# A Fourier mixer with a routed expert layer on one core: constant matmuls in TensorE's idle time, and one selection fewer

## The chip, the cores and the metric

One NeuronCore of a Trainium2 chip runs the whole program. The metric is device time in microseconds (us) for one execution, lower is better. Timings of the same program are repeated; the median of three runs stands for it.

## What is computed

For each of 8 batches, `x[b]` is a 3136 x 256 float32 array. It goes through a Fourier layer with a soft threshold, and then 128 of its 3136 rows go through an expert:

```python
X = rfft(x, axis=1)
Yr = Xr @ w_r - Xi @ w_i + b_r
Yi = Xr @ w_i + Xi @ w_r + b_i
Y = shrink(Yr, 0.01) + 1j * shrink(Yi, 0.01)
y = irfft(Y, n=3136, axis=1)
scores = y[b] @ w_gate
top = the 128 rows with the largest scores
out[b] = y[b]
out[b, top] += sigmoid(scores[top]) * (relu(y[b, top] @ w1) @ w2)
```

w1 is 256 x 1024 and w2 is 1024 x 256.

## The kernel before

**Stages of a batch.** 3136 is split as 98 x 32. In the first transform (`s1`, eight pieces a batch) DVE or POOL makes sums `xu` and differences `xv` of the input tile `xt`; TensorE (PE) multiplies them by the constant `first` into PSUM banks `s`; the result is stored to DRAM as `As`. In the second transform (`s2`, six passes a batch) PE multiplies the reloaded tile `av` by the constant `second` into `px0` and `px1`; ACT and DVE split the result into a high part `Xh` and a low part `Xl`. Eight spectral products (`spectral`, three matmuls each, with the weights `wh` and `wl`) follow each pass, into a bank `py`. `shrink` is the threshold. `s2i` (six a batch) and `s2it` transform back, and DVE takes the dot product with the gate at the same time (`score_part`, into `Csc`); the result goes to DRAM as `Cs`, comes back as `cin`, and eight `s1i` pieces a batch end the transform and store the output `out`.

**Routing.** `score(b)` brings a batch's scores into one tile. `select(bs, bits, lag)` (L516) finds the 128th largest score of each batch of a group by a search over the bits of the float: with bits = 3 there are twelve rounds. In a round DVE compares all scores with the candidates (tile `c`), counts (tile `n`), PE adds the counts over partitions by a product with ones (`px<-n,tm`), and DVE picks the digit from it (`digest`). Each step waits for the one before. After the last round come the mask, prefix sums on PE, one-hot rows (`hot`) and the row numbers `idxs`. `GROUPS` (L1032) says which batches are selected together; each group waits for the scores of all its batches and for the group before (`route`, L1088 to L1093).

**Expert.** For each batch POOL gathers 128 rows (`xe`, L643); PE turns them (`prepare`), multiplies by w1 in two halves of 16 matmuls (`hidden`), ACT and DVE make high and low parts, PE does 24 matmuls with w2 (`combine`), DVE adds (`ye`), and POOL scatters the rows (`out`, L723). Two threads of `ffn` can be at work after the last spectral product; before it, one.

**What sets the order.** The program is written out by a planner that runs while the kernel is built. It keeps a planned time for each engine (`free`), for each tile and for the DMA wire, and the order it writes is the order in which each engine's queue runs on the chip. `pe["end"]` is when PE's last planned matmul ends. The main loop (L1241 to L1295) takes, at each step, the PE work that costs least: a wait plus a penalty for being early or late in the plan (L1269 to L1273); selection and expert threads have a fixed rank, and `FIL` is the price of an expert step, first before and then after the end of the spectral products. `pump` writes the work of the other engines up to a planned time, which lies `AHEAD` (late in the program, `AHEADT`) in front of PE. `EARLY` lets a load from DRAM scratch be put in SP's queue that much before the store it needs is planned to land. `LOWA` and `DB` hold DVE's selection steps back while the spectral products run, `TD` does so for threads at the end (L1062 to L1072). `spec["t"]` counts passes of spectral products; T = 48 is all of them; `at` is 0 until the first product is written.

Of the kernel before, what the change touches and what calls it, by code (L numbers as in the profile page):

```python
# [10 lines left out]
F32 = mybir.dt.float32  # L11
# [8 lines left out]
B, S, D = 8, 3136, 256  # L20
# [141 lines left out]
def fourier_moe(ctx: ExitStack, tc: tile.TileContext, x, w_r, w_i, b_r, b_i, wg, w1, w2,  # L162
# [6 lines left out]
    ps = ctx.enter_context(tc.tile_pool(name="ps", bufs=2, space=bass.MemoryType.PSUM))  # L169
# [4 lines left out]
    free = dict.fromkeys(("PE", "DVE", "ACT", "POOL", "SP"), 0.0)  # L174
    done, read, base, where = {}, {}, {}, {}
    pe = {"mode": None, "end": 0.0}
# [81 lines left out]
    def mm(out, a, b, start=True, stop=True, at=(0, 0)):  # L258
        k, m, n = b.shape[0], out.shape[0], int(np.prod(b.shape[1:]))
        mode = (32 if k <= 32 else 64, 64) if k <= 64 and m <= 64 else (128, 128)  # L260
        t = begin("PE", [out], [a, b])
        if mode != pe["mode"]:
            t = max(t, pe["end"]) + 0.13
        c = max(n * (1.68 if b.dtype == F32 else 0.45), (220 if b.dtype == F32 else 110) if mode[0] == 128 else 28) / 1000
        own = [(r, q) for r in range(at[0] // 32, (at[0] + mode[0]) // 32) for q in range(at[1] // 32, (at[1] + mode[1]) // 32)]
        t = max([t] + [cells.get(x, 0.0) for x in own])
        for x in own:
            cells[x] = t + c
        pe["mode"], pe["end"] = mode, max(pe["end"], t + c)
        free["PE"] = max(free["PE"], t + 0.012)  # L270
        finish("PE", [out], [a, b], t + c + 0.15)
        return nc.tensor.matmul(out, a, b, start=start, stop=stop)  # L272
# [37 lines left out]
    def new(p, shape, dt, name, bufs=2):  # L310
        ring = rings.setdefault((name,), Ring(bufs))
        assert ring.bufs == bufs
        old = None
        if len(ring.tiles) >= bufs:
            old, holds = ring.tiles.pop(0)
            for g in holds:
                drain(g)
        t = p.tile(shape, dt, name=name, bufs=bufs)
        if old is not None:
            base[key(t)] = max(done.get(old, 0.0), read.get(old, 0.0))  # L320
        where[key(t)] = "ps" if p is ps else "sb"
        ring.tiles.append((key(t), []))
        return t

    def open_at(name, count=1):

        ring = rings.get((name,))
        if ring is None:
            return 0.0
        n = count - (ring.bufs - len(ring.tiles))  # L330
        t, v = 0.0, free["DVE"]
        for o, holds in ring.tiles[:max(n, 0)]:
            t = max(t, done.get(o, 0.0), read.get(o, 0.0))
            for s in holds:
                if not s.over:
                    v = max(v, s.when()) + 0.55
                    t = max(t, v)
        return t
# [66 lines left out]
    first = c_tile([128, 2, 2, 64], F32, "first")  # L405
# [3 lines left out]
    wh, wl = [c_tile([128, 2, 2, 2, D], F32R, n) for n in ("wh", "wl")]  # L409
# [27 lines left out]
    made = set()  # L437
# [5 lines left out]
    def consts_s():  # L443
        yield "SP", behind_a(CA[0])
        ld(sec[0].rearrange("p j s -> p (j s)"), t_second[:, :NJ * 64])
        yield "SP", behind_a(CA[3])
        ld(tail, t_tail)
        yield "SP", behind_a(CA[4])
        ld(wgb, wg.rearrange("(o e) -> o e", o=1).broadcast_to([128, D]))
        ld(sec[1].rearrange("p j s -> p (j s)"), t_second[:, NJ * 64:])  # L450

    def consts_w():
        yield "SP", behind_a(CA[1])
        ts = []
# [12 lines left out]
    def consts_bias():  # L467
        vec.memset(m2l, -2.0 * LAM)
        yield "SP", behind_a(CA[2])
        for c, src in enumerate((b_r, b_i)):  # L470
# [274 lines left out]
    def x_side():  # L745

        for b in range(B):
            for i in range(8):
                if b:
                    if b == 1:  # L750
                        yield "SP", behind_a(CA[5])
                    o = (b, i - XB) if i >= XB else (b - 1, i + (0 if b == 1 else XB))
# [262 lines left out]
    MX, SB = False, 4  # L1015
    Q = 6
    T = B * Q
    AVB = 2
    YP = (1,)
    R0 = 2  # L1020
    EARLY, AHEAD, SW = 0,1.1,0.2
    BACK, TAIL = 99,40
    LAST = 3
    PF = (0,0.3)
    BEGIN, RATE, DB = 2.5,2.2,0.3
    LOWA = 0.4
    AHEADT, FA, TD = 0.7,2,0.5
    BE, BU, BY = 99, 99, 1.0
    DG, GAP = 0.5,0.5
    STEP, THW, FIL = 5,4,(8,3)  # L1030
    END = 0.3
    GROUPS = ((0, 2), 2), ((2, 4), 2), ((4, 6), 3), ((6, 7), 3), ((7, 8), 3)  # L1032
    F1, I1 = [-1, 0, 0, 1, 2, 2, 3, 3],[10, 10, 11, 12, 12, 13, 14, 15]
    LEAD, LAG = 1.1,2.06
    NQ = 1
    CA = 1,2,8,9,10,9
    slots = {}
    spec = {"t": 0, "k": 0}
    s2n, s2m = {"t": 0}, {"t": 0}
# [48 lines left out]
    def route(bs, bits):  # L1088
        yield lambda: 0.0 if set(range(bs.start, bs.stop)) <= known else None

        yield lambda: 0.0 if bs.start == 0 or before[bs.start] in settled else None
        yield from select(bs, bits, lambda: 0.0 if spec["t"] >= T and bs.stop == B else LOWA - DB * owner[10 * bs.start - 200].behind())
        settled.update(range(bs.start, bs.stop))  # L1093
# [7 lines left out]

    before = {g[0][0]: h[0][0] for g, h in zip(GROUPS[1:], GROUPS)}

# [104 lines left out]
    def quad(t):  # L1208
        return divmod(t, Q)


    place1 = {}
    per = {}
# [8 lines left out]
    with tc.manual_schedule():  # L1222
        for t in xts + cts:
            vec.memset(t[:P0].rearrange("p a c -> p (a c)") if len(t.shape) == 3 else t[:P0].rearrange("p a c d -> p (a c d)"), 0.0)
        ld(first.rearrange("p z c s -> p (z c s)"), t_first)
        side(x_side())
        side(xsum_side())
        side(a_side())
        side(consts_s())
        side(consts_w())  # L1230
        side(consts_bias())
        side(consts_moe())
        side(c_side())
        side(csum_side())
        side(fetch())
        for bs, bits in GROUPS:
            spawn(route(slice(*bs), bits), 10 * bs[0] - 200, bs[1])
        spawn(ffn(False), 0)
        spawn(ffn(True), 0)
        spawn(rated(), -300)  # L1240
        while True:  # L1241
            now = max([free["PE"], min(cells.values(), default=0.0)])
            ahead = AHEAD if spec["t"] < TAIL else AHEADT
            pump(now + ahead)
            at = spec["t"] + spec["k"] / 8
            cands = []
            for f in (middle, forward, backward, forward1, backward1):
                c = f()
                if c:
                    cands.append(c)  # L1250
            for th in threads:
                if pe["mode"] != (128, 128) and cands and spec["t"] < T:
                    break
                w = th.when()
                if w is not None:
                    end = spec["t"] >= T
                    cands.append((FIL[end] if th.rank == 0 and not late() else th.rank * 0.001 - 2.0, w, th, "f"))
            if not cands:
                later = [s.when() for s in sides]
                later = [w for w in later if w is not None]  # L1260
                if not later:
                    break
                free["PE"] = max(free["PE"], min(later))
                pump(min(later))
                continue
            mode = "q" if pe["mode"] in ((32, 64), (64, 64)) else "f"
            best = None
            for c in cands:
                wait = max(c[1] - now, 0.0)  # L1269
                if isinstance(c[2], Thread):  # L1270
                    cost = THW * wait + c[0]
                else:
                    cost = wait + (STEP if spec["t"] < T else END) * max(c[0] - at, -1.0 if spec["t"] < T else -10.0) + (SW if c[3] != mode else 0.0)  # L1273
                if best is None or cost < best[0]:
                    best = cost, c
            c = best[1]
            if c[1] > now + 0.4:

                later = [s.when() for s in sides]
                later = [w for w in later if w is not None and w <= c[1]]  # L1280
                if later and min(later) > now + ahead:
                    free["PE"] = min(later) - ahead + 0.01
                    continue
            if isinstance(c[2], Thread):
                if c[2].rank < 0:
                    turned_at[0] = now
                elif spec["t"] >= T:
                    pump(max(now, c[1]) + FA)
                if PF[spec["t"] >= T]:
                    pump(max(now, c[1], free["DVE"]) + PF[spec["t"] >= T])  # L1290
                c[2].step()
                if c[2].over:
                    threads.remove(c[2])
            else:
                c[2]()  # L1295
        for s in list(sides):
            drain(s)
        assert not threads and spec["t"] == T and s2m["t"] == T
# [29 lines left out]
```

## Time and profile before

| | us |
|---|---|
| three runs | 711.32, 703.48, 709.24 |
| median | 709.24 |
| the profiled execution, device time | 712.16 |
| its span, first to last instruction | 710.4 |
| PE busy in the span | 656.2 (92%) |
| DVE / ACT / POOL busy | 417.5 / 360.9 / 393.5 |

The span is the time between the first and last instruction in the trace; 1.76 us of the profiled execution's time lie around it. PE's busy time counts an instruction at the length it had, so at half the clock the same work counts about double. PEclk is the granted clock: 1.00 is 2.4 GHz, 0.50 is 1.2 GHz.

### The profile page before, as it was taken

What the parts mean: (1) busy time and instruction counts of PE and PEld (TensorE: products, weight loads), DVE (VectorE), ACT (ScalarE), POOL (GpSimd) and SP (SyncE); (2) the same over time, 40 slices, a digit from 0 to 9 for tenths busy, and PEclk for the clock granted to TensorE, in tenths of its full rate; (3) what the DMA queues carried; (4) which work ended last, traced back from release to release, by engine and by line L of the source; (5) the groups of instructions that cost most, each with busy time, mean ns of one, the idle gap of its engine ahead of it and who ended that gap; (6) DMA issues with size and microseconds to landing.
All of it is one profiled execution on the core that took longest, in us unless ns stands there. A gap on an engine that the chain in (4) does not pass through costs nothing. (4 is left out here: it accounts for less than half of the span.)

```text
span 710.4 us, 19358 instructions
## 1 busy us (share of the span) xinstructions
PE 656.2 (92%) x7618; PEld 417.9 (59%) x7618; DVE 417.5 (59%) x1322; ACT 360.9 (51%) x766; POOL 393.5 (55%) x325
## 2 busy tenths in 40 slices
PE   4379999989999999989999999999998999998886
PEld 1046676656566655665566565665665665357786
DVE  7214454454366757674476677645776777577762
ACT  3326655655656565645665656565653545343111
POOL 5257645765867585747766666576452336253311
PEclk9769999999999999998999999999999999589999
DMA  8899778989798989986889898979883865593100
GB/s 243 270 275 304 255 235 262 254 258 293 224 259 258 324 292 272 298 279 194 197 317 278 291 224 303 274 246 213 230 266 110 192 189 151 153 272 114 39 22 23
DMA packets 85109, 162.54 MB, mean 229 GB/s; under 512 B 6333, under 2 KB 58906, under 8 KB 85018
## 3 DMA queue, kind: packets, MB, share of 16 engines
q1 hardware_dynamic: 83962, 159.13, 76.9%
q0 software_dynamic: 1056, 2.17, 1.1%
q8 instruction: 60, 0.98, 0.6%
q14 instruction: 31, 0.25, 0.1%
HBM read 83.23 MB, written 78.12 MB: 227 GB/s over the span
## 5 line engine op out<-in xcount | busy, mean ns | idle before, releaser
L272 PE MATMUL py<-wh,Xh 128*128 128x512 f32 x384 | 169.3, 441 | 1.6 <-DVE YT L220 1.1
L272 PE MATMUL py<-wl,Xh 128*128 128x512 f32 x384 | 151.8, 395 | 0.0
L272 PE MATMUL py<-wh,Xl 128*128 128x512 f32 x384 | 151.6, 395 | 0.0
L220 POOL TENSOR_TENSOR cu<-cin 113x512 f32<-113x512 f32 x56 | 72.2, 1290 | 102.5 <-PE s L272 89.2
L272 PEld LDWEIGHTS py<-wh,Xh 128*128 128x128 f32 x384 | 72.5, 189 | 92.5 <-issue 70.7
L220 POOL TENSOR_TENSOR xu<-xt 113x512 f32<-113x512 f32 x56 | 72.0, 1286 | 93.9 <-PE s L272 75.6
L220 DVE TENSOR_TENSOR Xl<-px,Xh 128x512 fp32r<-128x512 f32 x96 | 61.8, 685 | 87.6 <-ACT Xh L220 87.6
L220 DVE CUSTOM_DVE_ANT_0 junk<-s,wgb 128x256 f32<-128x256 f32 x192 | 80.6, 420 | 45.7 <-ACT ct L220 32.3
L220 ACT COPY ot<-s 113x512 f32<-113x512 f32 x136 | 72.9, 594 | 64.4 <-PE s L272 58.0
L220 POOL TENSOR_TENSOR cv<-cin 113x512 f32<-113x512 f32 x64 | 85.0, 1331 | 12.0 <-DMA cin<-Ct 7.6
L220 ACT COPY at<-s 113x512 f32<-113x512 f32 x120 | 64.4, 592 | 48.4 <-PE s L272 38.9
L272 PE MATMUL s<-xu,first 64*64 64x512 f32 (+1 forms) x256 | 76.3, 639 | 11.7 <-DVE xu L220 10.1
L220 POOL TENSOR_TENSOR xv<-xt 113x512 f32<-113x512 f32 x60 | 79.0, 1317 | 7.9 <-DMA xt<-in_x 6.7
L272 PEld LDWEIGHTS py<-wl,Xh 128*128 128x128 f32 x384 | 72.8, 190 | 16.8
L220 POOL TENSOR_TENSOR Y<-r,r 128x512 f32<-128x512 f32 x48 | 61.8, 1287 | 31.9 <-ACT r L220 22.6
L272 PE MATMUL s<-cu,first 49*64 49x512 f32 (+1 forms) x256 | 77.9, 651 | 1.5 <-DVE cu L220 1.5
L272 PEld LDWEIGHTS px<-second,av 64*64 64x64 f32 x3072 | 53.3, 138 | 43.7 <-DMA av<-As 18.0
L272 PEld LDWEIGHTS py<-wh,Xl 128*128 128x128 f32 x384 | 73.0, 190 | 9.2
L272 PE MATMUL px<-second,av 64*64 64x64 f32 x3072 | 59.0, 224 | 20.5 <-DMA av<-As 16.7
L272 PE MATMUL s<-cv,first 49*64 49x512 f32 (+1 forms) x256 | 76.6, 653 | 0.0
L220 ACT COPY ct<-s 128x256 f32<-128x256 f32 x192 | 57.6, 388 | 29.1 <-PE s L272 26.8
L272 PE MATMUL s<-xv,first 64*64 64x512 f32 (+1 forms) x256 | 71.9, 639 | 0.0
(127 smaller groups left out, 965.2 us busy)
## 6 DMA issues: line engine op xcount, KB each, us to landing
out<-ot SPq DMA_DIRECT2D x64, 392.0 KB
av<-As SPq DMA_DIRECT2D x48, 512.0 KB
Cs<-ct SPq DMA_DIRECT2D x48, 512.0 KB
cin<-Cs SPq DMA_DIRECT2D x64, 384.0 KB
xt<-in_x SPq DMA_DIRECT2D x60, 392.0 KB
As<-at SPq DMA_DIRECT2D x60, 392.0 KB
cin<-in_x SPq DMA_DIRECT2D x4, 392.0 KB
As<-ot SPq DMA_DIRECT2D x4, 392.0 KB
```

Of the source, the lines that this page charges most:

```text
L220: return f(*args, **kw)
L272: return nc.tensor.matmul(out, a, b, start=start, stop=stop)
```

## The change

`warm(t)` is called before each piece of work that the main loop writes, if the spectral products have all been written or none has. Where the plan has PE idle for at least 0.5 us before that work, it writes n matmuls on constants into a free bank (`s`, or else `py`), so many that they end 0.3 us before the work is planned to start. Nothing reads that bank's content. Their operands are `wh` once the weights are there (512 columns, planned at 0.23 us each), and the table `first` before that (float32, 256 columns, planned at 0.44 us each). The groups (6, 7) and (7, 8), of one batch each, become the group (6, 8) of two. Seven constants of the planner change.

```diff
-    EARLY, AHEAD, SW = 0,1.1,0.2
+    EARLY, AHEAD, SW = 0.6,1.1,0.2
...
-    BEGIN, RATE, DB = 2.5,2.2,0.3
-    LOWA = 0.4
-    AHEADT, FA, TD = 0.7,2,0.5
+    BEGIN, RATE, DB = 2.5,2.2,0.5
+    LOWA = 0.2
+    AHEADT, FA, TD = 1.3,2,0
...
-    STEP, THW, FIL = 5,4,(8,3)
+    STEP, THW, FIL = 5,4,(4,3)
...
-    GROUPS = ((0, 2), 2), ((2, 4), 2), ((4, 6), 3), ((6, 7), 3), ((7, 8), 3)
+    GROUPS = ((0, 2), 2), ((2, 4), 2), ((4, 6), 3), ((6, 8), 3)
...
+    WARM = (0.5, 0.3)
...
+    def warm(t):
+
+        t0 = pe["end"]
+        w = "w" in made
+        n = int((t - WARM[1] - t0) / (0.23 if w else 0.44))
+        if t - t0 < WARM[0] or n < 1:
+            return
+        for name, bufs in (("s", SB), ("py", 2)):
+            if open_at(name, bufs) <= t0 + 0.3:
+                o = new(ps, [128, 2 * D], F32, name, bufs)
+                free["PE"] = min(free["PE"], t0)
+                for _ in range(n):
+                    if w:
+                        mm(o, wh[:, 0, 0, 0, :128], wh[:, 0, 0].rearrange("p z d -> p (z d)"))
+                    else:
+                        mm(o[:, :D], first[:, 0].rearrange("p c s -> p (c s)"), first.rearrange("p z c s -> p (z c s)"))
+                return
...
+            if spec["t"] >= T or at == 0:
+                warm(c[1])
```

## Rows read from the trace of the kernel before

**Rows 1.** The page, part 2: the granted clock in 40 slices of 17.8 us.

```profile
PEclk9769999999999999998999999999999999589999
```

**Rows 2.** Stretches; columns: stretch, length, busy (count) of PE, PEld, DVE, ACT, POOL, PEclk, DMA share, GB/s.

```profile
48.00:600.00 552.00, 541.29 (x6806) 340.85 (x6806) 331.71 (x1065) 317.15 (x677) 337.18 (x280) 0.99 0.86 251
600.00:604.00 4.00, 2.44 (x38) 1.27 (x37) 1.93 (x8) 2.40 (x8) 3.80 (x4) 1.00 0.39 119
604.00:622.00 18.00, 17.02 (x82) 6.56 (x82) 9.09 (x44) 6.26 (x14) 4.93 (x4) 0.53 0.60 159
622.00:650.00 28.00, 25.26 (x168) 15.90 (x169) 20.54 (x52) 12.71 (x26) 15.04 (x10) 0.88 0.80 238
650.00:688.00 38.00, 32.48 (x268) 30.27 (x266) 28.18 (x112) 5.47 (x14) 7.81 (x8) 1.00 0.08 26
688.00:710.00 22.00, 16.32 (x121) 15.60 (x121) 6.92 (x24) 2.80 (x6) 3.22 (x4) 0.92 0.07 25
```

**Rows 3.** Stretches of one us near the start.

```profile
28.00:29.00 1.00, 0.00 (x0) 0.00 (x0) 0.00 (x0) 0.00 (x0) 0.00 (x0) 0.50 0.55 174
...
47.00:48.00 1.00, 1.00 (x3) 0.33 (x1) 0.00 (x0) 0.00 (x0) 1.00 (x1) 0.50 0.97 252
```

**Rows 4.** Timeline, first transforms; columns: start, length, what, [idle before <-releaser].

```profile
10.10 1.11 PE L272 MATMUL s<-xu,first 64*64 64x512 f32 x1 [10.10 <-DVE xu L220]
...
12.33 3.38 POOL L220 TENSOR_TENSOR xv<-xt 113x512 f32<-113x512 f32 x2 [1.15 <-PE s L272]
...
16.26 0.59 PE L272 MATMUL s<-xu,first 49*64 49x512 f32 x1
```

**Rows 5.** Timeline, the first pass of the second transform.

```profile
38.44 1.99 PE L272 MATMUL px<-second,av 64*64 64x64 f32 x64 [14.89 <-DMA av<-As]
...
42.04 1.96 PE L272 MATMUL s<-xu,first 64*64 64x512 f32 x2 [1.61 <-POOL xu L220]
```

**Rows 6.** Timeline, 600 to 618 us: a wait of PE, and batch 7's scores.

```profile
603.90 1.54 PE L272 MATMUL s<-Y,second 32*64 32x256 f32 x4 [1.56 <-DVE Csc L220]
...
617.01 0.19 DVE L220 COPY scores<-px 98x32 f32<-98x32 f32 x1 [1.62 <-PE px L272]
```

**Rows 7.** Timeline, DVE: counts of batches 6 and 7, and batch 7's indices.

```profile
601.15 0.39 DVE L220 TENSOR_REDUCE n<-c 98x7 bf16<-98x224 bf16 x1
...
644.64 0.19 DVE L220 TENSOR_REDUCE n<-c 98x1 bf16<-98x32 bf16 x1
...
651.46 0.19 DVE L220 TENSOR_REDUCE n<-c 98x1 bf16<-98x32 bf16 x1
...
684.62 0.19 DVE L220 TENSOR_REDUCE n<-c 98x1 bf16<-98x32 bf16 x1
...
692.88 0.15 DVE L220 TENSOR_TENSOR idxs<-col,px 128x1 uint32<-128x1 f32 x1
```

**Rows 8.** Groups by form, DVE: compare and count for one and for two batches.

```profile
L220 DVE TENSOR_REDUCE n<-c 98x7 bf16<-98x224 bf16 x20 | 7.8, 388 | 0.6
L220 DVE TENSOR_TENSOR c<-scores,px 98x224 bf16<-98x224 f32 x20 | 7.7, 383 | 0.4
...
L220 DVE TENSOR_TENSOR c<-scores,px 98x448 bf16<-98x448 f32 x10 | 6.2, 619 | 0.2
L220 DVE TENSOR_REDUCE n<-c 98x14 bf16<-98x448 bf16 x10 | 6.2, 618 | 0.3
```

**Rows 9.** Timeline, DVE: one-hot rows of the pair 4 and 5, batch 4's first.

```profile
574.87 0.29 DVE L220 TENSOR_SCALAR hot<-iota,row 98x128 f32<-98x128 f32 x1
...
576.04 0.28 DVE L220 TENSOR_SCALAR hot<-iota,row 98x128 f32<-98x128 f32 x1
```

**Rows 10.** Timeline, the last expert pass, batch 7.

```profile
697.58 0.38 PE L285 MATMUL py<-ident,xe 128*128 128x128 f32 x2
...
698.65 3.84 PE L272 MATMUL py<-xT,w1s 128*128 128x128 f32 x32 [0.69 <-DVE xT L220]
...
705.57 0.48 DVE L220 SCALAR_TENSOR_TENSOR ye<-py,ga,xe 128x256 f32<-128x256 f32 x1 [1.66 <-PE py L272]
```

## The prediction

> **What bounds the kernel now.** I read the page's slices first, then a table of stretches, then the timeline where the clock changes, then DVE's selection steps, and last the end of the chain.
>
> In the slices the granted clock is at 9 or 10 tenths except twice: two slices near the start and two or three from about 600 us [rows 1]. The table of stretches says what kind of place each is. From 48 to 600 us PE is busy 541.29 of 552 us at a clock of 0.99 [rows 2]: that stretch is bound by PE, with 10.7 us of idle time in all, and whatever is added to it on PE costs its length. The DMA share there is 0.86, so loads are not far behind. From 600 us it is another program: PE is busy 2.44 + 17.02 + 25.26 + 32.48 + 16.32 = 93.5 of 110.4 us, but 17.02 of these run at a granted clock of 0.53 and 25.26 at 0.88 [rows 2].
>
> The first low stretch comes after PE has had nothing to do. The first second-stage pass waits 14.89 us for the load of `av` [rows 5]; by 28 us the clock is at 0.50 and at 47 us, with PE at work again, it still is [rows 3]. The second comes at 604 us, after short batched matmuls and a wait of 1.56 us for DVE [rows 6].
>
> The end is set by selection. Batch 6's counts run from 601.15 to 644.64 us, seven of them, so six gaps of 7.2 us; batch 7's begin only then, twelve from 651.46 to 684.62, eleven gaps of 3.0 us [rows 7], though batch 7's scores stood at 617.2 [rows 6]. So 34 us pass in which batch 7 waits for batch 6 (`route` asks for the group before). From batch 7's indices at 693.03 to the end of the span are 17.4 us [rows 7, 10]. Under these chains PE does the expert passes of batches 0 to 6.
>
> **The change, part by part.**
>
> *Constant matmuls before the first transform.* PE's first work starts at 10.10 us [rows 4]; the plan sees idle time there, and from its own constants it would write about twelve float32 matmuls (an estimate: a planned first sum near 5.7 us, less 0.3, by 0.44). On the chip they start when `first` has landed and must be over by 10.10 to cost nothing. One pass over 512 columns took 1.11 us at 10.10 us and 0.59 us at 16.26 [rows 4], so the engine ran at about half rate at first, though the first slice of the clock line reads 9 tenths [rows 1]. A float32 matmul of 256 columns costs about what that row does: twelve at the fast rate are 7 us, at the slow one 13. What can be won is small, since after this POOL sets the pace: its third difference waited 1.15 us for PE [rows 4]. Between +3 us (they end late) and -1.1 us I take -0.5.
>
> The Trainium skill (TensorE: Matmul & The Clock Gate, "Part 1: The HAM clock gate") says that the throttled state is the default and that matmuls release it, so that whatever comes first runs at the low rate; by that rule most of the early fillers are slow themselves and speak against this part. The two lengths above agree. By the rule alone the term would be near its upper end of +3 us, by the POOL row -1.1.
>
> *Constant matmuls before the second transform.* The idle 14.89 us before 38.44 us [rows 5] would be filled with products of `wh`. If the clock is then up at 38.44, PE's work from there to the end of the low stretch, past 47 us [rows 3], shrinks. But the second-stage matmuls would end early only to wait again: the next work waits for POOL until 42.04 [rows 5]. From there to some 48.8 us, 6.8 us at half rate, PE has work, so at most 3.4 us are won. If the fillers end too early the clock is down again and nothing is won; if the plan's idle time is longer than the chip's they push the pass back, by perhaps 2 us. I take -2.0 (-3.4 to +2). Both start terms: -2.5. As PE is busy from 48 to 600 us, time won here is carried to the end.
>
> *Constant matmuls after the spectral products.* If they hold the clock at 1.00, each stretch's busy time shrinks by its missing share: 17.02 x 0.47 = 8.0, 25.26 x 0.12 = 3.0, 16.32 x 0.08 = 1.3, together 12.3 us [rows 2]. That is the most that clock alone gives, with the 16.9 us of idle time in the 110.4 left as they are (the fillers lie in idle time, so they add nothing if they lie where PE really is idle). Bounds: 0 (the clock falls as before) and -12.3. I take all 12.3, because the waits of PE in this part are short (1.56 us is among the longest [rows 6]) and just such waits are what is filled. PE's sum for the tail is then 710.4 - 12.3 = 698.1.
>
> A filler is also a wait: it needs its bank's readers to be done, and PE is in order, so all PE work is queued behind it. If the plan is early by 1 us against the chip, the filler holds up work that was ready. DVE and ACT, which wait for PE, then wait too. This is priced in the rivals.
>
> *Batches 6 and 7 together.* Removed: batch 6's twelve rounds and its end, and the 34 us in which batch 7 waits. Added: each round of the joint chain compares and counts 448 elements in place of 224, 0.619 + 0.618 against 0.383 + 0.388, so +0.47 us a round [rows 8]; a second batch's one-hot rows, 576.04 - 574.87 = 1.2 us [rows 9]; and batch 6's expert pass, which so far lay under batch 7's selection, now comes after it, behind the same indices.
>
> The joint chain's length: it can start when batch 7 is scored, 617.2 [rows 6]; at full clock the steps before it (604 to 617) shorten, of at most 6 us I take 3: 614.2. One us to the first count. Eleven gaps of g. From the last count to the indices 693.03 - 684.62 = 8.4 us [rows 7], with the second batch 10. From the indices to the end 17.4. Then the second expert pass: PE's share of one is from 697.58 to 705.57 without the 0.69 of waiting and the last matmul's way to DVE, 7.2 us [rows 10]; its gather runs beside the first. The end is at 614.2 + 1 + 11 g + 10 + 17.4 + 7.2 = 649.8 + 11 g.
>
> For g the rows give 3.0 + 0.47 = 3.5 (batch 7's, with expert passes in between) and 7.2 (batch 6's, at half clock, beside the last `s1i` pieces and their sums on DVE) [rows 7, 8]. The last `s1i` pieces stay, so I take 5 for the first five gaps and 3.5 for the six after that: 46 us, a mean of 4.2. The end is then at 696.0. Nothing is gained in PE's sum by this, but it is what allows PE's sum to be reached: PE's 698.1 ends after the chain's 696.0, so the later of the two holds and the tail is -12.3.
>
> *The constants* (EARLY, DB, LOWA, AHEADT, TD, FIL) move work within queues. A price of 4 in place of 8 may put expert passes in among the spectral products, where PE is full: 7.2 us of PE time there for 7.2 less at the end, nothing in sum. EARLY lets a load stand in SP's queue before its data is there, and the loads and stores behind it on SP wait with it; between 48 and 600 us all such effects together have 10.7 us of idle PE to win [rows 2] and as much to lose. The value I take is 0, with 3 either way, since the idle time there is 2% and spread thin.
>
> **The sum.** -2.5 - 12.3 = -14.8 us. Against the profiled execution: 712.16 - 14.8 = 697.4. That execution lay 2.9 us above the median of the runs shown; on the median, 709.24 - 14.8 = **694.4 us**, 2.1% faster. A measurement of this kernel can tell about 1% from no change, here 7.1 us.
>
> **Rivals.**
>
> *The joint chain goes at batch 6's pace.* Then the end is late: 649.8 + 11 g passes the old 710.4 at g = 5.5, and with the 2.5 us of the start at 5.7. At g = 6.5 it is 721.3, with the start 718.8, which is +8.4: 717.6 us on the median. For it: batch 6's gaps of 7.2, two expert passes with nothing left to hide them, and DVE busy 20.54 of 28 us from 622 to 650 [rows 2]. Against: the slow gaps lay in the low clock, and DVE loses batch 6's rounds. Chance 0.12.
>
> *The fillers don't hold the clock, or stand where PE isn't idle.* Then the 12.3 is lost or paid back: the plan's waits are not the chip's. Chain 696.0 plus the lost 3 us and about 0.6 us a gap more for the slower PE gives 705.6, and PE's sum stays near the old one less a few us of idle time: some 707, so -3.4, and with half the start term -4.7: 704.5 us on the median, no change that can be told. For it: the idle time in the tail comes from many short waits, each planned with model times; against: PE has idle time enough (16.9 us) to absorb fillers. Chance 0.20.
>
> *Better than forecast:* all gaps at 3.5 and the idle time in the tail halved beyond the 4.9 us after the last matmul (about 6 us): the chain ends at 688.3, PE at 692.1, together with -3.4 at the start -21.7: 687.5 us. Chance 0.15.
>
> **How the numbers follow.** Forecast 0.53, better 0.15, no gain 0.20, slower 0.12. Faster by over 1% (below 702.1): the first two and a little of the third, 0.70. Within 1%: 0.18. Slower by over 1% (above 716.3): 0.12. The range takes the better case with 5 us to spare on the constants and reaches over the no-gain case to the edge of the slow one: 682 to 712. The forecast's own range, from the start term's +1 and the clock's 9 us to the full terms, is 688 to 702.
>
> **What would show it.** Right: a clock of 1.00 from 600 us on; fillers from 24 to about 36 us and a second-stage pass of 1.1 in place of 1.99 us; twelve counts of 98x14 for batches 6 and 7, the first within 3 us of batch 7's scores and gaps of 3.5 to 5 us; indices near 669 us and two gathers behind each other; last matmul near 690 us. Wrong: a clock of 0.50 after 604 us; gaps over 5.5 us; PE rows that wait for a bank a filler holds; a later first transform than 10.10 us; more idle PE between 48 and 600 us than 10.7 us.

## The result, and the profile after

The changed kernel takes 700.62 us, median of 14 runs (690.91 to 703.44), against 708.56 (703.48 to 712.72, 14 runs) for the kernel before: ratio 0.9857, 95% interval 0.9822 to 0.9893. The medians count all runs; the ratios, here and below, leave out runs more than 1.5% above the quickest of their kernel. By the medians the gain is 7.9 us, a little over half of the 14.8 forecast (10.1 us by the ratio), and the time is inside the range. The profiled execution was a quick one: 699.05 us, 1.6 below its median, with a span of 696.9, where the one before lay 3.6 above its own. So the traces differ by 13.1 us, of which 5.2 belong to the choice of the two executions.

The page of the changed kernel, parts 1 and 2:

```profile
PE 672.4 (96%) x7733; PEld 433.6 (62%) x7733; DVE 403.9 (58%) x1231; ACT 360.1 (52%) x766; POOL 392.9 (56%) x325
...
PEclk9989999999999999999999999999999999989999
```

PE has 115 instructions more than the 7618 before (131 constant matmuls, called fillers from here on, less 16 that the joint selection of batches 6 and 7 saves), and is busy 16 us longer in a shorter span. The two dips of [rows 1] are shallower. Stretches of the changed kernel, as in [rows 2] (stretch, length, busy and count of PE, PEld, DVE, ACT, POOL, granted clock, DMA share, GB/s):

```profile
48.00:600.00 552.00, 542.91 (x6815) 342.45 (x6817) 329.74 (x1054) 319.71 (x685) 336.02 (x279) 0.99 0.86 253
...
604.00:622.00 18.00, 16.47 (x82) 7.95 (x86) 9.66 (x24) 6.12 (x12) 10.68 (x8) 0.81 0.89 248
622.00:650.00 28.00, 26.80 (x189) 18.87 (x185) 24.43 (x66) 8.93 (x18) 10.58 (x8) 1.00 0.47 139
650.00:688.00 38.00, 35.91 (x299) 34.16 (x297) 17.41 (x57) 6.75 (x18) 8.10 (x9) 1.00 0.10 34
```

The same clock times don't hold the same work in both kernels, so I cut both traces at two points of the program: the load of batch 1's `avt`, and the start of the first `s<-Y,second` matmul behind the last spectral product. Before, they are at 123.41 and 600.3 us, after at 121.51 and 590.1. The difference of 13.5 us between the spans thus falls into three parts: 1.9 us up to the first point (forecast 2.5), 8.3 between the points (forecast 0) and 3.3 in the tail behind the second (forecast 12.3). In these two executions the total is near; the shares are not. The first of them is also no more than executions differ by: the kernels below without a filler at the start reach this point at 120.92 to 124.65 us.

The start. Timeline of PE in the changed kernel (start, length, what, [idle before <-releaser]):

```profile
2.97 7.93 PE L272 MATMUL s<-first 128*128 128x256 f32 x24 [2.97 <-DMA first<-t_first]
10.83 0.64 PE L272 MATMUL s<-xu,first 64*64 64x512 f32 x1
...
23.73 10.71 PE L272 MATMUL py<-wh 128*128 128x512 f32 x46 [0.36 <-DVE wh L220]
...
35.18 1.16 PE L272 MATMUL px<-second,av 64*64 64x64 f32 x64 [0.74 <-DMA av<-As]
```

The first transform starts 0.7 us later than in [rows 4], behind the fillers, but each of its matmuls takes 0.64 in place of 1.11 us. The second-stage pass takes 1.16 in place of the 1.99 of [rows 5], and it comes 3.3 us earlier because `av` did (at 37.41 us, 1.0 us earlier, in a kernel with no filler at all, e6 below).

The selection. DVE in the changed kernel: batch 7's scores, the first and last of twelve joint counts, the indices:

```profile
602.54 0.19 DVE L220 COPY scores<-px 98x32 f32<-98x32 f32 x1 [0.96 <-PE px L272]
...
603.03 0.22 DVE L220 TENSOR_REDUCE n<-c 98x2 bf16<-98x64 bf16 x1
...
653.46 0.22 DVE L220 TENSOR_REDUCE n<-c 98x2 bf16<-98x64 bf16 x1
...
663.25 0.16 DVE L220 TENSOR_TENSOR idxs<-col,px 128x2 uint32<-128x2 f32 x1
```

Against [rows 6, 7] the scores come 14.5 us earlier, and one chain of eleven gaps, (653.46 - 603.03) / 11 = 4.6 us each, stands where two chains stood. The indices are there at 663.25, not at 692.88. But the span ends 33.7 us behind them, where it was 17.5. POOL's gathers (`xe`) for batches 6 and 7 and the last scatter show why:

```profile
664.21 0.97 POOL L643 DMA_INDIRECT xe<-out,idxs  x1 [0.94 <-issue]
673.57 0.96 POOL L643 DMA_INDIRECT xe<-out,idxs  x1 [8.39 <-DVE ye L220]
...
692.89 0.97 POOL L723 DMA_INDIRECT out<-ye,idxs  x1 [6.48 <-DVE ye L220]
```

Batch 7's gather waits 8.39 us for an earlier expert pass to give up its tile. From 650 to 688 us PE is busy 35.91 of 38 us, with those passes and 12 fillers of 3.9 us: the end is set by the passes that PE still has to do, not by selection.

### The profile page after: what moved, and what is told of

Read it like the earlier page. It is cut to its first block, busy times and chain, and to the rows that moved or that the text cites. A ratio compares the mean times of both kernels' runs of the same rounds, so it can differ in the third digit from the quotient of the medians.

```text
span 696.9 us, 19479 instructions
## 1 busy us (share of the span) xinstructions
PE 672.4 (96%) x7733; PEld 433.6 (62%) x7733; DVE 403.9 (58%) x1231; ACT 360.1 (52%) x766; POOL 392.9 (56%) x325
## 4 chain that ended last, share of the span: by engine, by line
PE 78%; DMA 7%; DVE 6%; issue 5%; ACT 1%; POOL 1%; SPq 0%; POOLq 0%; DVEq 0%; ACTq 0%
PE py L272 43%; PE s L272 26%; PE px L272 9%; DMA cin<-Ct 1%; DMA cin<-Cs 1%; DMA xe<-in_moe_w 1%; DVE px L220 1%; DVE r L220 1%; DMA As<-ot 1%; DMA xt<-in_x 1%; DVE c L220 1%; DMA av<-As 1%; DMA As<-at 1%; DVE junk L220 1%; POOL out L723 0%
## 5 line engine op out<-in xcount | busy, mean ns | idle before, releaser
L272 PE MATMUL s<-cu,first 49*64 49x512 f32 (+1 forms) x256 | 76.5, 621 | 2.2 <-DVE ok L220 1.5
L272 PE MATMUL s<-xu,first 64*64 64x512 f32 (+1 forms) x256 | 71.4, 620 | 1.6 <-POOL xu L220 1.6
L272 PE MATMUL s<-cv,first 49*64 49x512 f32 (+1 forms) x256 | 71.8, 624 | 0.0
L272 PE MATMUL s<-xv,first 64*64 64x512 f32 (+1 forms) x256 | 70.0, 623 | 0.0
L220 ACT CAST Xh<-px 128x512 fp32r<-128x512 f32 x96 | 51.7, 593 | 34.2 <-PE px L272 33.9
```

The source lines that it names most:

```text
L220: return f(*args, **kw)
```

## The experiments

Each kernel ran beside the kernel before on the same chip; ratios are to that. Two theories stood at first: that the fillers gain time (by the clock), or that they cost it and the gain comes from the joint selection and the constants.

**e1_no_fill: the change without the fillers.**

```diff
-            if spec["t"] >= T or at == 0:
-                warm(c[1])
```

> The whole change without its constant matmuls (selection of 6 and 7 together and the seven constants stay). If the fillers are worth what the clock rows of before and after say (about 2 us at the start and 7 us of low clock in the tail), this loses most of the gain: 705 to 709 us where the kernel before has 708.6, the clock at 0.50 for some 15 us after the last spectral product. If the gain comes from the joint selection and the constants, it stays near the change's 700.6 us, 699 to 702.

Measured: 693.57 us, 0.9771 (0.9737 to 0.9805). The interval lies wholly below that of the change: the fillers cost 6 us by the ratios and 7 by the medians.

**e2_mute: fillers planned as before, but only the first of each group written.** The order of everything else stays that of the change.

```diff
-                for _ in range(n):
+                for i in range(n):
...
+                        mm(o, wh[:, 0, 0, 0, :128], wh[:, 0, 0].rearrange("p z d -> p (z d)"), emit=i == 0)
```

> Every group of constant matmuls is planned as in the change, so the order of all other work is the same, but only the first matmul of each group is written. If the fillers work by holding the clock, the time goes up to 704 to 708 us and the clock rows look like those of before. If they work by changing the order that the planner writes, it stays at 699 to 702 us. If they stand in the way of ready work in the tail (idle time without fillers grew from 16.9 to 23.3 us there), it is faster, under 698 us.

Measured: 693.64 us, 0.9794 (0.9757 to 0.9832). So it is not the changed plan that costs, but the matmuls themselves. The same run tells of the clock. Two stretches of the changed kernel, 10 to 30 us behind the second cut:

```profile
600.18:610.18 10.00, 9.87 (x58) 4.51 (x50) 3.00 (x11) 5.28 (x10) 7.47 (x6) 1.00 0.74 206
610.18:620.18 10.00, 8.47 (x37) 4.25 (x37) 6.66 (x17) 2.24 (x5) 6.84 (x4) 0.66 0.85 238
```

And the same stretches of the mute kernel:

```profile
597.73:607.73 10.00, 9.11 (x48) 2.79 (x39) 3.01 (x11) 5.27 (x10) 7.44 (x6) 1.00 0.76 212
607.73:617.73 10.00, 8.51 (x36) 4.30 (x36) 6.59 (x18) 2.42 (x5) 7.29 (x4) 0.66 0.90 242
```

The clock is 1.00 and then 0.66 in both, with the fillers and nearly without. Timeline of PE in the changed kernel, where it falls:

```profile
608.97 1.41 PE L272 MATMUL py<-wh 128*128 128x512 f32 x5
611.91 0.81 PE L272 MATMUL s<-cu,first 64*64 64x512 f32 x1 [1.53 <-DVE ok L220]
```

The fillers end at 610.4, and then PE waits 1.53 us for DVE all the same: the planner had put them into an idle time that it saw, and the one that the chip had came behind it. (DVE itself was held there by a `cu` that waited 2.5 us for its load.)

**e3_old_groups: the change, batches 6 and 7 selected separately.** The planner then writes 58 fillers into the tail, not 42.

```diff
-    GROUPS = ((0, 2), 2), ((2, 4), 2), ((4, 6), 3), ((6, 8), 3)
+    GROUPS = ((0, 2), 2), ((2, 4), 2), ((4, 6), 3), ((6, 7), 3), ((7, 8), 3)
```

> The change with batches 6 and 7 selected one after the other, as before. If the joint selection carries the tail, the end is late again by some 6 to 10 us: 706 to 710 us. If PE's sum bounds the tail whatever the selection does, only the few us of PE and DVE work of twelve rounds are lost: 701 to 704 us.

Measured: 707.67 us, 0.9985 (0.9958 to 1.0011): the joint selection is worth 7 us within this change. DVE in this kernel, indices of batch 6, the next count, the indices of batch 7:

```profile
639.09 0.15 DVE L220 TENSOR_TENSOR idxs<-col,px 128x1 uint32<-128x1 f32 x1
639.52 0.19 DVE L220 TENSOR_REDUCE n<-c 98x1 bf16<-98x32 bf16 x1
...
683.70 0.15 DVE L220 TENSOR_TENSOR idxs<-col,px 128x1 uint32<-128x1 f32 x1
```

The two chains stand behind each other as in [rows 7], and the tail is 110.0 us long, as before (110.1), against 106.8 in the change. That is 3.2 of the 7 us; the other half lies ahead of the tail in these two executions (595.0 against 590.1), where the orders hardly differ, and I can't assign it.

**e4_old_consts: the change with the seven constants of before.** (The diff is the constants' part of the change, turned round.)

> The change with the old seven constants. The prediction took them at nothing, with 3 us either way: 698 to 704 us. If the 8 us that the profile of after gains between 48 and 590 us come from them, 706 to 709 us.

Measured: 709.53 us, 0.9990 (0.9957 to 1.0023): 9 us slower than the change. I had priced the constants at nothing.

**e5_change_again and e6_no_fill_again:** the change and the kernel of e1 on another chip, side by side.

> The change itself once more, beside the three kernels below on one chip. If the fillers really cost time, it lies at 698 to 703 us and the kernel without fillers 5 us or more below it in the same rounds. If the difference between the first result and the run without fillers came from the chip or the day, both are within 2 us of each other.

> The change without its constant matmuls, beside the change. If the fillers cost time: 692 to 696 us, 5 to 7 below the change. If not: within 2 us of it.

Measured: 701.33 us, 0.9862 (0.9820 to 0.9905), and 693.40 us, 0.9773 (0.9740 to 0.9805). The cost of the fillers stands. In the tail of the kernel without a filler, the stretch behind the second cut (begun 0.2 us ahead of it),

```profile
586.60:689.60 103.00, 86.73 (x670) 64.09 (x667) 59.70 (x177) 30.31 (x67) 35.65 (x28) 0.96 0.37 110
```

the clock is 0.96 and the length 103.0 us, while the change has

```profile
590.00:696.90 106.90, 96.56 (x711) 71.85 (x709) 59.68 (x177) 30.39 (x67) 35.23 (x28) 0.94 0.36 106
```

The change has 9.8 us more of PE time there: 13.1 us of fillers (below), less 3.3 us by which its other work is shorter. Its tail is 3.9 us longer all the same, and its mean clock is no better. Before, this stretch had a clock of 0.88 (600.3 to 710.4 us); most of the rise needs no filler.

**e7_fill_start and e8_fill_tail: fillers only ahead of the first spectral product, or only behind the last.**

```diff
-            if spec["t"] >= T or at == 0:
+            if at == 0:
```

> The change with constant matmuls only before the first spectral product. In the profiles so far these win 1 to 2 us by 120 us. If the cost lies in the tail's fillers, this is the best so far: 691 to 693 us. If it lies at the start or in what fillers do to the whole run, 698 to 702.

```diff
-            if spec["t"] >= T or at == 0:
+            if spec["t"] >= T:
```

> The change with constant matmuls only after the last spectral product. If the tail's fillers stand in the way of ready work: 697 to 702 us. If they cost nothing (the muted and the full fillers had the same clock by stretch, and the tail differed by 1.8 us): 693 to 696.

Measured: 701.41 us, 0.9885 (0.9837 to 0.9933), and 694.76 us, 0.9774 (0.9737 to 0.9812). The start fillers carry the whole cost; the tail's change nothing that can be told. That is the reverse of what the prediction had: it gave the tail 12.3 us and the start 2.5, both to the good. The tail's fillers do shorten its other work: in e8 it is 93.1 us of PE time less 13.0 of fillers, 80.1, against 86.6 in e6. But time without work grows from 16.3 to 24.2 us, and the tail is no shorter (104.3 against 102.8 us).

**e9_short_start: as many start fillers, each over 8 columns.**

```diff
+                        mm(o, wh[:, 0, 0, 0, :128], wh[:, 0, 0].rearrange("p z d -> p (z d)"), cut=None if spec["t"] >= T else 8)
```

> The change with the same number of constant matmuls before the first spectral product, in the same places of the same order, but each over 8 columns in place of 256 or 512; those of the tail as in the change. If the start's fillers cost by the time that they take in front of ready work or by what their clock does, this is as fast as the kernel without them: 692 to 696 us. If the cost comes from the added instructions (the waits of PE at 218, 300 and 557 us that no other engine ends), it stays at 698 to 703 us.

Measured: 705.40 us, 0.9938 (0.9907 to 0.9970), slower than with full columns. So what costs is not the time that the columns take. (Its profiled execution took 699.36 us, 6 us under its median, so its trace shows little of this cost.) Its timeline:

```profile
23.48 6.23 PE L272 MATMUL py<-wh 128*128 128x8 f32 x46
...
36.05 1.99 PE L272 MATMUL px<-second,av 64*64 64x64 f32 x64 [6.34 <-DMA av<-As]
```

The 46 short ones took 6.23 us (46 of full length: 10.71), PE then waited 6.34 us for `av`, and the pass behind took 1.99 us: the work for the clock is gone, the instructions are there. In the groups by form (operation, tiles, shape, count | busy us, mean ns | idle before), the change has

```profile
L272 PE MATMUL py<-wh 128*128 128x512 f32 x66 | 17.7, 418 | 0.4 <-DVE wh L220 0.4
L272 PE MATMUL s<-wh 128*128 128x512 f32 x27 | 8.6, 421 | 0.0
L272 PE MATMUL s<-first 128*128 128x256 f32 x24 | 7.9, 507 | 3.0 <-DMA first<-t_first 3.0
L272 PE MATMUL py<-first 128*128 128x256 f32 x14 | 4.6, 424 | 0.0
```

Of the change's 131 fillers, 42 (27 and 15 with `wh`; 8.6 and 4.5 us, together 13.1) lie in the tail, 89 at the start.

**e10_old_lowa and e11_old_early: no fillers, and of the constants only LOWA = 0.4 and DB = 0.3, or only EARLY = 0, as before.**

```diff
-    BEGIN, RATE, DB = 2.5,2.2,0.5
-    LOWA = 0.2
+    BEGIN, RATE, DB = 2.5,2.2,0.3
+    LOWA = 0.4
```

> The change without constant matmuls and with the old LOWA and DB (0.4 and 0.3), which hold DVE's selection steps back while spectral products run. If these two constants carry the 8 us of the constants: 700 to 704 us. If not: 692 to 695.

> The change without constant matmuls and with the old EARLY (0), which decides where a load stands in SP's queue. If it carries the constants' 8 us: 700 to 704 us. If not: 692 to 695; with e10 also there, the rest lies in AHEADT, TD and FIL.

Measured: 707.00 us, 0.9979 (0.9953 to 1.0006), and 692.79 us, 0.9780 (0.9749 to 0.9811). Without the fillers LOWA and DB together are worth 13.6 us; EARLY alone changes nothing that can be told. AHEADT, TD and FIL were not taken back alone. The traces show what LOWA and DB do. Both hold DVE's selection steps back. DVE and POOL in the kernel with the old values:

```profile
310.69 1.35 DVE L220 SCALAR_TENSOR_TENSOR hot<-iota,end,hot 98x128 f32<-98x128 f32 x1
...
311.85 1.33 POOL L220 TENSOR_TENSOR xu<-xt 113x512 f32<-113x512 f32 x1
311.96 1.30 DVE L220 TENSOR_SCALAR hot<-iota,row 98x128 f32<-98x128 f32 x1
...
314.80 0.35 DVE L220 SCALAR_TENSOR_TENSOR hot<-iota,end,hot 98x128 f32<-98x128 f32 x1
...
315.65 1.28 DVE L220 TENSOR_TENSOR Xl<-px,Xh 128x512 fp32r<-128x512 f32 x2
316.39 1.08 PE L272 MATMUL px<-row,hot 98*128 98x34 f32 x8 [1.11 <-DVE Xl L220]
...
319.35 0.79 PE L272 MATMUL py<-wh,Xh 128*128 128x512 f32 x1 [1.10 <-DVE YT L220]
```

Eight one-hot steps stand in front of `Xl`. Three of them take about 1.3 us in place of 0.3, those beside POOL's additions. `Xl` is late, PE waits twice for 1.1 us, and then pays again. Stretches of the same kernel:

```profile
315.00:320.00 5.00, 2.78 (x15) 1.94 (x14) 4.14 (x14) 0.69 (x1) 1.06 (x1) 0.89 0.80 292
320.00:325.00 5.00, 5.00 (x23) 1.71 (x25) 1.68 (x7) 1.43 (x3) 2.87 (x3) 0.50 0.23 70
```

After a stretch with PE busy 2.78 of 5 us, the next five run at 0.50, in the part of the program that PE bounds. With the new values the same one-hot steps still take up to 1.41 us, but they stand where nothing of PE's waits for them, and the stretch in which their product runs is

```profile
305.00:310.00 5.00, 5.00 (x96) 3.86 (x94) 1.79 (x7) 2.34 (x5) 4.42 (x5) 1.00 0.93 341
```

The waits of PE from 62 us to the end of the spectral products (waited for: total us, times, longest), old values without fillers:

```profile
PE px L272 <- DVE n L220: 2.5, 1, 2.5
...
PE px L272 <- DVE hot L220: 2.1, 3, 1.2
...
PE px L272 <- DVE Xl L220: 1.1, 1, 1.1
PE py L272 <- DVE YT L220: 1.1, 1, 1.1
```

and new values without fillers (e6):

```profile
PE px L272 <- DVE c L220: 1.7, 3, 0.6
PE px L272 <- DVE mask L220: 0.9, 1, 0.9
```

No wait over 0.9 us is left. Between the two cuts, with one matmul's difference in the work, old values and then new values (without fillers):

```profile
120.92:601.25 480.33, 467.93 (x5725) 291.13 (x5718) 291.53 (x938) 271.97 (x581) 293.21 (x235) 0.98 0.85 247
121.79:586.78 464.99, 459.80 (x5726) 288.27 (x5718) 288.29 (x938) 271.70 (x582) 293.27 (x235) 1.00 0.87 255
```

Idle time falls from 12.4 to 5.2 us, and busy time by 8.1 us.

The Trainium skill (GPSIMD Engine Reference, "1. Specifications") says that GpSimd shares its SBUF interfaces with VectorE and that they contend where a VectorE instruction has two SBUF inputs or runs in a two-port mode; the step `hot<-iota,end,hot` reads two tiles in SBUF, and its 0.35 and 1.35 us above agree; that the step `hot<-iota,row` runs in a two-port mode is not shown here. On the clock, the skill (TensorE: Matmul & The Clock Gate, "HAM oscillation — how this bites in real kernels") tells of short groups of matmuls between waits that leave the next group throttled; 2.78 of 5 us and then 0.50 agree, though the page's waits are for loads and longer than the work between them, and here two waits of 1.1 us were enough.

**e12_wh_only: the change without the fillers on `first`.** The 46 on `wh` at the start become 53 and end only when `av` is there; the tail's stay.

```diff
-        if t - t0 < WARM[0] or n < 1:
+        if t - t0 < WARM[0] or n < 1 or not w:
```

> The change without the 38 constant matmuls on the table first (those up to 24 us); the 51 on wh before the first spectral product and those of the tail stay. If the cost goes with the number of added instructions at the start (0 of them 693 us, 89 of them 701), it lies between: 696 to 699 us. If the ones on first cost it all: 692 to 695. If the wh ones cost it all: 699 to 703.

Measured: 696.48 us, 0.9847 (0.9811 to 0.9883), between e6 and the change, though its interval overlaps that of the change. By the count of fillers written at the start, the medians are 693.4 us for 0, 693.6 for 16 (e2), 696.5 for 55 (here), 701 for 89 (the change) and 705.4 for 89 short ones. They rise with the count, but the count alone doesn't fix them.

**How they cost.** Two things appear in the traces with start fillers. The first is a wait of PE that no other engine ends. In the changed kernel, timeline of PE:

```profile
218.34 0.65 PE L272 MATMUL s<-Y,second 32*64 32x256 f32 x5 [0.95 <-issue]
...
557.41 1.25 PE L272 MATMUL px<-second,av 64*64 64x64 f32 x41 [2.44 <-issue]
```

and in e9, with the short ones:

```profile
219.24 0.65 PE L272 MATMUL s<-Y,second 32*64 32x256 f32 x5 [0.94 <-issue]
...
557.21 0.81 PE L272 MATMUL px<-second,av 64*64 64x64 f32 x41 [1.55 <-issue]
```

They stand at the same two instructions, hundreds of us behind the last start filler, and again in e5 (0.67 and 1.78 us) and e7 (0.94 and 1.80, and 0.83 at a third). e3 has the first (0.96) and two others (1.29 and 0.57), e4 two elsewhere (0.82 and 0.98), and e12 one of 1.41 at a neighbour of the second. Between the cuts the profiled executions of the kernels without start fillers (before, e1, e6, e8, e10, e11) have none, and e2, with 16, has one of 0.83 us.

What PE waits for there can be read from the traces. The page has a DMA queue for instructions; in the change and in e6:

```profile
q8 instruction: 61, 1.00, 0.6%
...
q8 instruction: 60, 0.98, 0.6%
```

In each kernel's trace it brings one packet of 16 KB to every 256 of PE's instructions (a matmul and its weight load are two). All 16 waits above are at one place in that count, before an instruction whose number is 193 above a multiple of 256 (number 5,057 at 218.34 us, number 13,505 at 557.41), and end 1.29 to 1.66 us after such a packet landed. In the kernels without start fillers the packets landed 4.6 to 8.0 us ahead of the same numbers. So PE waits there for its own instructions, and fillers at the start shift which of its work stands at such a place. Why the packet comes late there is open. A wait of this kind can cost clock too: behind the one of 2.44 us the granted clock is 0.50 from 557.6 to 561.0 us.

The second is that the start got irregular. PE in e5, the change's other execution:

```profile
39.94 1.99 PE L272 MATMUL px<-second,av 64*64 64x64 f32 x64 [5.05 <-DMA av<-As]
...
96.56 1.16 PE L272 MATMUL px<-second,av 64*64 64x64 f32 x64 [2.03 <-DMA av<-As]
```

Here `av` came at 39.9 us, 5.05 us behind the last filler; the clock was down again and the pass took 1.99 us, as without fillers. Batch 1's `av` was late too, PE waited 2.03 us, and the clock fell to 0.50 from 98 us on. This execution was at the first cut 8.3 us behind the one shown above (129.85 against 121.51) and took 705.5 us. Six runs of e5 spread over 8.7 us, six of e6 over 2.8, so I take such draws to be part of the median's 7 us; that is argued, not shown, and six runs of e1, the same kernel as e6, spread over 10.6. The "issue" waits are 2 to 4 us of the some 7 with 89 fillers: between the cuts the change is as busy as e6 (460.3 and 459.8 us) and 3.1 us longer idle (8.3 and 5.2). How much of the rest the late loads are, single executions don't tell. A start with 128 matmuls more, one whole packet, which by this reading would leave the places where they were, was not run.

The best version is the change without fillers: 693.40 us, where the change beside it had 701.33 and the kernel before 708.88. Not tried: each part alone on the kernel before, and LOWA and DB one by one.

## Why the prediction was right, and where its steps failed

The direction was right, and the time is inside the range (700.62 in 682 to 712), with a little over half of the gain that was forecast. The sum came out of other terms than those it was made of: that their errors of both signs left it there is luck. Against the change (by medians), whose two values of 700.62 and 701.33 I take as 700.8, taking out the fillers gives -7.4 us, taking out the joint selection +6.9 and the constants +8.7. These need not add up in another order: without fillers LOWA and DB are worth 13.6.

*Constant matmuls at the start, -2.5.* In the profiled execution -1.9 us stood at the first cut, but e6, with no filler, was there 1.6 us ahead of the kernel before as well, so a gain by the fillers isn't shown. Both passes ran faster, as forecast; the first fillers were slow, as forecast too (507 ns each, against 424 for the later ones on the same table; start to start 0.43 us up to 8 us, 0.22 from there on). There were 24 of them and not twelve, but they took 7.93 us, 0.33 each, where the prediction had 0.58 to 1.1. The step that failed is "As PE is busy from 48 to 600 us, time won here is carried to the end." It holds only if what comes later isn't touched; e7 and e8 put the cost of these fillers at some 7 us, with new waits for "issue" and loads that vary. And "If the fillers end too early the clock is down again and nothing is won", named as a condition, is what e5 (5.05 us early) and e7 (3.08) show; in the profiled execution it was 0.74.

*Constant matmuls behind the spectral products, -12.3.* The condition "If they hold the clock at 1.00" was met in part at best: 0.66 in the same place with and without them (e2), and no gain in time in e8 against e6, where they shorten the work and the waits grow. Their reason, "just such waits are what is filled", failed at 611 us: the fillers filled the plan's idle time, PE waited behind them. The 3.3 us that the tail did shrink are the joint selection's (e3 has the old length with all its fillers). Of its 110.1 us before, 93.2 were work; after, 96.6 - 13.1 = 83.5 are, so work fell by 9.7 us, of which 6.6 fall without any filler (86.6 in e6), and time without work grew from 16.9 to 23.3. The rival "The fillers don't hold the clock, or stand where PE isn't idle", at 0.20 and 704.5 us, describes this part better than the forecast.

*Batches 6 and 7 together, no gain by itself.* The chain was well sized: gaps of 4.6 for 4.2, indices at 663.25 for some 669, since the scores came at 602.5 and not at 614. That PE's sum and not the chain sets the end was right too. The term was booked at nothing by itself, as what "allows PE's sum to be reached", and this half e3 bears out: undone, batch 7's indices come at 683.70 us again and 7 us are lost. What is seen of it is the tail's 3.2 us.

*The constants, 0 with 3 either way.* "The value I take is 0, with 3 either way, since the idle time there is 2% and spread thin" is, beside the tail's 12.3, the term most mis-sized: 8.7 us, and LOWA and DB are the only ones found to matter (13.6 without fillers). The idle 10.7 us were taken for all that could be won. But a wait of 1 or 2 us can also halve the clock for the next us of work (0.50 from 320 to 325 us in e10), so that PE's busy time holds a loss as well: between the cuts e10 is busy 467.9 of 480.3 us and e6 459.8 of 465.0. Idle time fell by 7.2 us and busy time by 8.1. And EARLY, of the two constants that I worked through, does nothing that can be told; FIL was not tried alone.

## What to carry to other kernels

Before adding matmuls to hold the clock, run the kernel with all of them planned and only the first of each group written: if the clock in the doubtful place is the same, they don't do their work, and what they cost is seen beside it. In a stretch that PE bounds, count each wait of PE together with the clock in the few us behind it: a handful of waits of one or two us, removed by two constants that hold DVE back, were worth more here than all fillers. Take a change of several parts apart one by one before believing its sum; here three terms of 7 to 9 us with two signs made a plausible 8. And matmuls that are added can move all later ones against the packets in which PE's instructions come.

## What the runs showed of the hardware that I had not expected

- Instructions added at the start made PE wait for "issue" hundreds of us later (16 waits of 0.57 to 2.44 us in eight kernels), with full and with 8 columns alike, each at the same place in a count of 256 of PE's instructions and 1.29 to 1.66 us behind the landing of a 16 KB packet of instructions.
- VectorE's one-hot step over 98 x 128 elements takes 0.27 to 0.35 us alone and 1.26 to 1.41 beside POOL's additions, a factor of four.
- A float32 matmul over 8 columns is hardly cheap: at a granted clock of 1.00 they start 0.112 us apart (e9), where those over 512 columns start 0.227 apart (the change); at 0.50 the short ones start 0.213 apart.
